# Capped attention and two MLPs on one core: first pair reordered on ScalarE, one tiny load moved to another queue, two pairs' sums moved behind accumulating transfers

## The chip, the cores and the metric

The kernel runs on one core of a Trainium2 chip. The metric is the device time of one execution in microseconds (us). Three runs of the kernel before took 581.67, 581.72 and 582.16 us, median 581.72. TensorE (PE in the profile), VectorE (DVE), ScalarE (ACT), GpSimd (POOL) and SyncE (SP) each run their own instruction stream in order; SP, ACT and POOL issue DMAs, each on its own queue.

## The reference

```
scores = cap * tanh((q @ k.T / sqrt(64)) / cap)          # 2 batches x 12 heads, 448 tokens
attn   = exp(scores - max); attn = attn / sum(attn)       # per row
x  = (attn @ v) as 896 x 768
h  = x @ w_in;  x = (h * sigmoid(1.702 h)) @ w_out        # 768 -> 2048 -> 768
xn = x / rms(x) * rms_g
y  = (silu(xn @ w_gate) * (xn @ w_val)) @ w_out2          # 768 -> 1536 -> 768
```

All inputs are float32. cap is one number that is loaded at run time.

## The kernel before

The attention works on 12 pairs of heads, `p` = 0 to 11; pairs 0 to 5 are the first batch, 6 to 11 the second. A pair's 448 keys are cut into three chunks of 128 and a rest of 64 ("the shared chunk", in which the two heads share the partitions). For each chunk TensorE makes scores (`scores`, `first_scores`, `scores_last`), ScalarE takes tanh (`tanh`, scale `tsc`, which VectorE makes from the loaded `cap` in `scale_by_cap`) and then exp in place (`exp`, scale `capt`). Chunks 0 and 1 stand in a tile `pa`, chunk 2 and the shared chunk in a tile `pb`. `outputs` multiplies with v into one PSUM tile, `copy_out` copies that to `z`.

Row sums: VectorE adds chunks 0 and 1 into `ts` (`add_two`); for pairs 1 to 9 GpSimd issues two accumulating DMAs (`add_third`, L340) that add the shared chunk into `ts`. `sums` (L349 to L368) lets TensorE multiply `ts` and then chunk 2 of `pb` with ones, 4 products for each stream (pairs without the DMAs have a third stream with `blk`), and VectorE transposes, takes reciprocals (`few`) and transposes back (`rs`). `spread` (L370) copies `rs` by four DMAs into a tile `r` with a row for each output row; SP issues all four, for pair 11 two of them go by ACT's queue. `norm` is three instructions on VectorE: `z` times `r` (L378), the rounded high half of the MLP's input `x` (L383), and the low half (L390). For pairs 10 and 11 ScalarE makes the high half (L385).

What sets the order is the program text: one loop over `p` (L435 to L504) in which each engine's instructions are written out, with tables `plan`, `RAW` and `NORMS` for the decoding and loading of weights and for the norms. Sums of a pair run two loops later (`done_`, L483), the last ones behind the loop's end. Buffers come from rotating pools: 3 `ts`, 4 `pb`, 2 `rs`, 5 `r`, 3 score tiles in PSUM, 1 output tile.

Behind it the MLP runs as one stream of TensorE products, three for each block (L568 high x high, L569 high x low, L570 low x high weights). Its first two columns use tokens 0 to 383 (pairs 0 to 5), the next two tokens 384 to 895, so pairs 6 to 11. Weights are loaded in units; each is decoded on ScalarE and VectorE into a `ring` tile, high half by L155 on ScalarE, low half by L160 on VectorE. Units 0 and 1 are ready early; unit 2's rest and unit 3 are decoded right behind the last norm. Four steps of the last norm and of unit 2 are handed to the MLP (`norm_last`) so that they stand in this order: `norm_mul(11)`, `norm_hi(11)`, L143 of unit 2, `norm_lo(11)`.

Of the kernel before, what the change touches and what calls it, by code (L numbers as in the profile page):

```python
# [12 lines left out]
ALU = mybir.AluOpType  # L13
# [4 lines left out]
def attn_moe_kernel(  # L18
# [14 lines left out]
    nc = tc.nc  # L33
# [9 lines left out]
    NC = 3  # L43
    NPR = B * NP
# [8 lines left out]
    capt = keep.tile([128, 1], F32, name="capt")  # L53
# [120 lines left out]
    def attention():  # L174
        with ExitStack() as actx:
# [15 lines left out]
            xs, raws, vs, pa, pb, zt, nr, ts_ = {}, {}, {}, {}, {}, {}, {}, {}  # L191
# [15 lines left out]
            cuts = [slice(0, S), slice(64, 192), slice(192, XW - S), slice(0, 64)]  # L207
# [86 lines left out]
            def exp(t):  # L294
                nc.scalar.activation(out=t, in_=t, func=AF.Exp, scale=capt)  # L295
# [31 lines left out]
                    nc.vector.tensor_copy(z, ps)  # L327

            LAST = range(1, NPR - 2)

            def add_two(p):
                ts_[p] = ap_.tile([128, 2, S], F32, tag="ts", name="ts", bufs=3)
# [2 lines left out]
            def add_third(p):  # L335
                if p == NPR - 1:
                    nc.vector.tensor_tensor(out=ts_[p], in0=ts_[p], in1=pb[p][:, 0:2], op=ALU.add)  # L337
                elif p in LAST:
                    for j in range(2):
                        nc.gpsimd.dma_start(  # L340
                            out=ts_[p][half[j], :, j * SH:(j + 1) * SH],
                            in_=pb[p][half[j], 2].rearrange("p (e s) -> p e s", e=2), accum_op=ALU.add,
                        )

            def sums(p):
                ps = ps_s.tile([128, 2, 512], F32, tag="s", name="s")[:, 0]
                streams = [ts_[p], *([] if p == NPR - 1 else [pb[p][:, 0:2]]), *([] if p in LAST else [None])]
                for n, some in enumerate(streams):
                    for e in range(2):  # L349
                        for j in range(2):  # L350
                            if some is None:
                                w, t = blk[:, 64 * j:64 * j + 32], pb[p][:, 2, e * SH:(e + 1) * SH]
                            else:
                                w, t = f(ones)[:, 0:32], some[:, e, j * SH:(j + 1) * SH]
                            r0 = 64 * j + 32 * e
                            nc.tensor.matmul(  # L356
                                out=ps[r0:r0 + 32, 0:SH], lhsT=w, rhs=t,
                                start=(n == 0), stop=(n == len(streams) - 1), skip_group_check=True,
                            )
                by_token = zrp.tile([128, SH // 32, 32], F32, tag="bt", name="bt", bufs=2)  # L360
                nc.vector.transpose(out=by_token.rearrange("p b t -> p (b t)"), in_=ps[:, 0:SH])
                few = zrp.tile([128, SH // 32], F32, tag="few", name="few", bufs=2)
                nc.vector.reciprocal(out=few, in_=by_token[:, :, 0])
                nr[p] = zrp.tile([128, SH], F32, tag="rs", name="rs", bufs=2)
                nc.vector.transpose(
                    out=nr[p], in_=few.rearrange("p (b o) -> p b o", o=1).to_broadcast([128, SH // 32, 32]),
                )
# [30 lines left out]
            nc.vector.memset(f(xA[0][:, 0, 0:S]), 1.0)  # L398
            ts = first_kq()
            nc.scalar.dma_start(out=ts[0], in_=q[0])  # L400
            nc.scalar.dma_start(out=capt, in_=cap.rearrange("(o n) -> o n", o=1).to_broadcast([128, 1]))
            nc.scalar.activation(out=tiny, in_=f(ones)[:, 0:1], func=AF.Tanh)
            nc.sync.dma_start(out=ts[1], in_=k[0, :, cuts[1]])
            nc.sync.dma_start(out=ts[2], in_=k[0, :, cuts[2]])
            nc.sync.dma_start(out=ts[3], in_=k[0, :, cuts[3]])
            constants()
            load_kq(1)
# [27 lines left out]
            for p in range(NPR + 1):  # L435
                load_kq(p + 3 if p < 2 else p + 4)
                load_v(p + 2)
                if p == 1:
                    load_kq(5)
                if p in RAW:  # L440
                    load_to(RAW[p])
                if p == 0:
                    for c in range(NC):
                        if c:
                            scores(0, c)
                            tanh(0, c)
                        else:
                            first_scores()
                        if c < 2:
                            exp(pa[0][:, c])  # L450
                    scores_last(0)
                    tanh(0, NC)
                    exp(pb[0])
                    outputs(0, (0,))
                    split_kq(1)
                    scores(1, 0)
                    outputs(0, (1,))
                elif p < NPR:
                    for c in range(NC):
                        if c and p == 1:  # L460
                            scores(p, c)
                        tanh(p, c)
                subtract = cast_kq(p + 2) if p + 2 < NPR else None
                for n in NORMS.get(p, (p - 6,) if p >= 6 else ()):
                    norm(n)
                decode(p, "b")
                if subtract:
                    subtract()
                decode(p, "c")
                if p >= 1:  # L470
                    if p == NPR:
                        sums(p - 2)
                        spread(p - 2)
                        add_third(p - 1)
                    if p < NPR:
                        outputs(p - 1, (NC,))
                        scores_last(p)
                        outputs(p - 1, range(NC) if p > 1 else (2,))
                    else:
                        outputs(p - 1)  # L480
                    if p < NPR:
                        copy_out(p - 1, "D")
                    done_ = p - 1 if p == 1 or p == NPR else p - 2  # L483
                    if done_ not in nr:
                        if p == NPR:
                            norm(8)
                        sums(done_)
                        if p == NPR:
                            copy_out(p - 1, "A")
                        spread(done_)  # L490
                        if p == NPR:
                            norm(9)
                if 1 <= p < NPR:
                    tanh(p, NC)
                    exp(pa[p])
                    exp(pb[p])
                if p < NPR:
                    add_two(p)
                    decode(p, "d")
                    if p < NPR - 1:  # L500
                        add_third(p)
                if p >= 1:
                    for c in range(NC):
                        scores(p + 1, c)  # L504
# [377 lines left out]
```

## Time and profile before

| what | value |
|---|---|
| median of three runs | 581.72 us |
| the profiled execution's own time | 581.83 us |
| its span in the profile | 580.0 us |
| granted TensorE clock | 1.00 |
| PE busy | 572.7 us, 99% |
| DVE busy | 411.9 us, 71% |
| ACT busy | 274.1 us, 47% |
| POOL busy | 59.1 us, 10% |
| chain that ended last, by engine | PE 94%, ACT 3%, DVE 1%, DMA 1% |

The share of busy time is a mean over stages with different limits. In the first 80 us, the attention, ACT has no idle time; from 84.6 us on only the MLP's products run on PE. A matmul's end in the trace is modelled, so starts are the better reading. PEld is the load of weights into PE.

### The profile page before, as it was taken

How to read it: one execution, taken by the hardware profiler on the slowest of the kernel's cores; microseconds unless marked ns; L12 is line 12 of the kernel's file. 1: busy time of each engine (PE TensorE's matmuls, PEld its weight loads, DVE VectorE, ACT ScalarE, POOL GpSimd, SP SyncE). 2: the span in 40 equal slices, each digit the busy share in tenths (PEclk: the TensorE clock that was granted, in tenths of full speed). 3: DMA queues.
4: the chain of work that ended last, by engine and by line, in shares of the span. 5: the costliest groups of instructions: out<-in, count | busy, mean ns of one | idle time of the engine just before them, and what ended most of it. 6: DMA issues, size and time to landing. Idle time of an engine off the chain costs nothing.

```text
span 580.0 us, 9373 instructions
## 1 busy us (share of the span) xinstructions
PE 572.7 (99%) x3842; PEld 493.2 (85%) x3842; DVE 411.9 (71%) x568; ACT 274.1 (47%) x369; POOL 59.1 (10%) x54
## 2 busy tenths in 40 slices
PE   8899999999999999999999999999999999999997
PEld 4566668989999998999998989889898998989887
DVE  4889997956653355656787999873687894778732
ACT  7999965755241355553444543442233431334300
POOL 0222300000000000000222013000222000222000
PEclk9999999999999999999999999999999999999999
DMA  8888643642624123233142414351132361222022
GB/s 300 245 218 198 123 113 90 201 135 94 206 62 157 56 71 127 98 124 120 61 148 70 164 59 160 110 164 54 55 114 104 111 217 56 61 108 105 1 92 99
DMA packets 60363, 70.31 MB, mean 121 GB/s; under 512 B 4128, under 2 KB 56480, under 8 KB 60320
## 3 DMA queue, kind: packets, MB, share of 16 engines
q1 hardware_dynamic: 57136, 67.04, 35.4%
q0 software_dynamic: 2592, 2.07, 3.0%
q10 hardware_dynamic: 592, 0.61, 0.4%
q8 instruction: 30, 0.49, 0.3%
q14 instruction: 13, 0.11, 0.1%
HBM read 62.13 MB, written 2.75 MB: 112 GB/s over the span
## 4 chain that ended last, share of the span: by engine, by line
PE 94%; ACT 3%; DVE 1%; DMA 1%; issue 0%; ACTq 0%
PE b L570 28%; PE b L569 28%; PE b L568 28%; PE v L314 4%; PE s L246 3%; PE s L356 1%; ACT pa L292 1%; PE s L273 1%; ACT pb L292 1%; ACT pb L295 1%; DMA capt<-in_cap 1%; ACT pa L295 1%; DVE ts L333 0%; DVE ts L337 0%; PE b L707 0%
## 5 line engine op out<-in xcount | busy, mean ns | idle before, releaser
L570 PE MATMUL b<-x,ring 128*128 128x384 f32 (+1 forms) x480 | 173.9, 362 | 0.0
L569 PE MATMUL b<-x,ring 128*128 128x384 f32 (+1 forms) x480 | 173.8, 362 | 0.0
L568 PE MATMUL b<-x,ring 128*128 128x384 f32 (+1 forms) x480 | 173.7, 362 | 0.0
L568 PEld LDWEIGHTS b<-x,ring 128*128 128x128 f32 x480 | 90.1, 188 | 9.9 <-issue 0.4
L569 PEld LDWEIGHTS b<-x,ring 128*128 128x128 f32 x480 | 90.1, 188 | 9.6
L570 PEld LDWEIGHTS b<-x,ring 128*128 128x128 f32 x480 | 90.1, 188 | 9.4
L160 DVE TENSOR_TENSOR ring<-dec,ring 128x768 fp32r<-128x768 f32 x68 | 77.1, 1136 | 28.1 <-ACT ring L155 28.1
L570 PE MATMUL b<-g,ring 128*128 128x512 f32 (+1 forms) x192 | 69.7, 363 | 0.0
L569 PE MATMUL b<-g,ring 128*128 128x512 f32 (+1 forms) x192 | 69.6, 363 | 0.0
L568 PE MATMUL b<-g,ring 128*128 128x512 f32 (+1 forms) x192 | 69.5, 362 | 0.0
L155 ACT ACTIVATE ring<-dec 128x768 fp32r<-128x768 f32 x66 | 55.2, 837 | 30.0 <-DVE dec L143 24.5
L143 DVE SCALAR_TENSOR_TENSOR dec<-raw,dec 128x768 uint32<-128x768 uint32 x68 | 66.8, 983 | 1.2
L137 DVE SCALAR_TENSOR_TENSOR dec<-raw,dec 128x768 uint32<-128x768 uint32 x68 | 64.7, 952 | 1.0
L129 ACT ACTIVATE dec<-raw 128x768 f32<-128x768 f32 x66 | 59.6, 904 | 5.0 <-issue 2.5
L570 PE MATMUL b<-uA,ring 128*128 128x512 f32 (+1 forms) x144 | 52.1, 362 | 0.0
L569 PE MATMUL b<-uA,ring 128*128 128x512 f32 (+1 forms) x144 | 52.1, 362 | 0.0
L568 PE MATMUL b<-uA,ring 128*128 128x512 f32 (+1 forms) x144 | 52.1, 362 | 0.0
L600 DVE TENSOR_TENSOR g<-gg,g 128x384 fp32r<-128x384 f32 (+1 forms) x32 | 20.0, 624 | 39.9 <-ACT g L597 39.8
L739 POOL TENSOR_TENSOR a<-a,gg 128x512 f32<-128x512 f32 (+1 forms) x18 | 29.2, 1621 | 187.1 <-DVE gg L732 160.0
L742 ACT ACTIVATE uA<-a 128x512 fp32r<-128x512 f32 (+1 forms) x24 | 13.9, 580 | 70.4 <-POOL a L739 52.1
L133 DVE TENSOR_SCALAR dec<-dec 128x768 uint32<-128x768 uint32 x68 | 39.4, 580 | 0.0
L569 PEld LDWEIGHTS b<-g,ring 128*128 128x128 f32 x192 | 36.0, 188 | 3.9
(89 smaller groups left out, 664.4 us busy)
## 6 DMA issues: line engine op xcount, KB each, us to landing
raw<-in_moe_w_out SPq DMA_DIRECT2D x20, 768.0 KB, 4.2
raw<-in_moe_w_in SPq DMA_DIRECT2D x16, 768.0 KB, 4.5
raw<-in_moe_w_gate SPq DMA_DIRECT2D x12, 768.0 KB, 4.2
raw<-in_moe_w_val SPq DMA_DIRECT2D x12, 768.0 KB, 4.2
raw<-in_moe_w_out SPq DMA_DIRECT2D x8, 512.0 KB, 3.6
v<-in_v SPq DMA_DIRECT2D x11, 256.0 KB, 5.2
r<-rs SPq DMA_DIRECT2D x46, 56.0 KB, 2.6
kq<-in_k SPq DMA_DIRECT2D x11, 224.0 KB, 4.6
```

Source lines behind the costliest of these rows:

```text
L129: nc.scalar.activation(out=f(d), in_=f(hi), func=AF.Copy, scale=2.0 ** -112)
L133: nc.vector.tensor_scalar(out=d, in0=d, scalar1=3, scalar2=None, op0=ALU.logical_shift_left)
L137: nc.vector.scalar_tensor_tensor(out=d, in0=hi, scalar=0x80000000, in1=d, op0=ALU.bitwise_and, op1=ALU.bitwise_or)
L143: nc.vector.scalar_tensor_tensor(out=d, in0=lo, scalar=29, in1=d, op0=ALU.logical_shift_right, op1=ALU.bitwise_or)
L155: nc.scalar.activation(out=t[:, 0], in_=f(dec_t[w][0]), func=AF.Copy)
L160: nc.vector.tensor_tensor(out=t[:, 1], in0=f(d), in1=f(t[:, 0]), op=ALU.subtract)
L314: nc.tensor.matmul(out=ps[32 * n:32 * n + 32, j, 0:SH], lhsT=w[:, d0:d0 + 32], rhs=t, start=not before, stop=len(before) == NC, skip_group ...
L568: nc.tensor.matmul(out=wide(o, b), lhsT=w0, rhs=x0, start=first, stop=False)
L569: nc.tensor.matmul(out=wide(o, b), lhsT=w0, rhs=x1, start=False, stop=False)
L570: nc.tensor.matmul(out=wide(o, b), lhsT=w1, rhs=x0, start=False, stop=last)
L600: nc.vector.tensor_tensor(out=gA[1].at(i, hb), in0=gg[0], in1=f(gA[0].at(i, hb)), op=ALU.subtract)
L739: eng.tensor_tensor(out=t[0], in0=t[0], in1=t[1], op=ALU.mult)
```

## The change

1. The first pair on ScalarE: tanh of chunk 1 now stands ahead of exp of chunk 0, and exp of chunk 1 behind tanh of chunk 2 and of the shared chunk. TensorE makes all three score chunks of pair 1 ahead of `outputs(0, (1,))`.
2. The load of `cap` moves from ACT's queue to SP's, second there, and the third piece of the first k (`ts[2]`, 128 KB) from SP's to ACT's, second there.
3. For pairs 8 and 9 GpSimd issues a third accumulating DMA, which adds chunk 2 (128 x 896 numbers) to `ts`; it names the same bytes as the two ahead of it and is issued once they have landed. `sums` of these pairs then has one stream of 4 products instead of two.
4. The sums of pair 8 move from loop 10 to loop 11, those of pair 9 from loop 11 behind those of pair 10 in loop 12. In loop 12 VectorE's `add_third(11)` and TensorE's `outputs(11, (0, 1))` come first. In loop 10 the condition on `done_` now gives 0, which is no longer in `nr`, so `sums(0)` and `spread(0)` run a second time there; nothing reads their result.

```diff
+            BOTH = (8, 9)
...
                             in_=pb[p][half[j], 2].rearrange("p (e s) -> p e s", e=2), accum_op=ALU.add,
                         )
+                    if p in BOTH:
+                        nc.gpsimd.dma_start(out=ts_[p], in_=pb[p][:, 0:2], accum_op=ALU.add)
...
-                streams = [ts_[p], *([] if p == NPR - 1 else [pb[p][:, 0:2]]), *([] if p in LAST else [None])]
+                streams = [ts_[p], *([] if p == NPR - 1 or p in BOTH else [pb[p][:, 0:2]]), *([] if p in LAST else [None])]
...
-            nc.scalar.dma_start(out=capt, in_=cap.rearrange("(o n) -> o n", o=1).to_broadcast([128, 1]))
+            nc.scalar.dma_start(out=ts[2], in_=k[0, :, cuts[2]])
...
-            nc.sync.dma_start(out=ts[2], in_=k[0, :, cuts[2]])
+            nc.sync.dma_start(out=capt, in_=cap.rearrange("(o n) -> o n", o=1).to_broadcast([128, 1]))
...
-                    for c in range(NC):
-                        if c:
-                            scores(0, c)
-                            tanh(0, c)
-                        else:
-                            first_scores()
-                        if c < 2:
-                            exp(pa[0][:, c])
+                    first_scores()
+                    scores(0, 1)
+                    tanh(0, 1)
+                    exp(pa[0][:, 0])
+                    scores(0, 2)
+                    tanh(0, 2)
                     scores_last(0)
                     tanh(0, NC)
+                    exp(pa[0][:, 1])
                     exp(pb[0])
                     outputs(0, (0,))
                     split_kq(1)
-                    scores(1, 0)
+                    for c in range(NC):
+                        scores(1, c)
                     outputs(0, (1,))
...
                     if p == NPR:
-                        sums(p - 2)
-                        spread(p - 2)
                         add_third(p - 1)
+                        outputs(p - 1, (0, 1))
+                        for n in (p - 2, p - 3):
+                            sums(n)
+                            spread(n)
...
-                        outputs(p - 1)
+                        outputs(p - 1, (2, NC))
...
-                    done_ = p - 1 if p == 1 or p == NPR else p - 2
+                    done_ = p - 1 if p in (1, NPR) else p - 3 if p == NPR - 1 else p - 2 if p < NPR - 2 else 0
```

In the program after the change the lines behind the edits stand 3 lower (L356 is L359, L378 is L381).

ScalarE at the start of the kernel, pair 0, before (`first` are the pieces of q and k, L262 the tanh of chunk 0 in two halves, L295 exp):

```order
L400 DMA first_93<-in_q 128x448
L401 DMA capt<-in_cap 128x1
L402 ACT_TABLE_LOAD
L402 ACTIVATE tiny<-ones 128x1
L205 DMA v<-in_v 128x512
L262 ACTIVATE pa<-s,tsc 128x2x224 x2
L295 ACTIVATE pa<-pa,capt 128x896
L292 ACTIVATE pa<-s,tsc 128x896
L295 ACTIVATE pa<-pa,capt 128x896
L292 ACTIVATE pb<-s,tsc 128x896
L292 ACTIVATE pb<-s,tsc 128x448
L295 ACTIVATE pb<-pb,capt 128x1344
```

The same place now:

```order
L403 DMA first_93<-in_q 128x448
L404 DMA first_95<-in_k 128x256
L405 ACT_TABLE_LOAD
L405 ACTIVATE tiny<-ones 128x1
L205 DMA v<-in_v 128x512
L262 ACTIVATE pa<-s,tsc 128x2x224 x2
L292 ACTIVATE pa<-s,tsc 128x896
L295 ACTIVATE pa<-pa,capt 128x896
L292 ACTIVATE pb<-s,tsc 128x896
L292 ACTIVATE pb<-s,tsc 128x448
L295 ACTIVATE pa<-pa,capt 128x896
L295 ACTIVATE pb<-pb,capt 128x1344
```

No exp follows directly on the tanh that it reads; the load of `cap` left this queue and a piece of k came.

TensorE at the attention's end, from the products of pair 10 with v on, before (`ts_1130` is pair 9, `ts_1235` pair 10, `ts_1336` pair 11):

```order
L314 MATMUL v_1269<-pb_1160,v_942 32x224 x8
L356 MATMUL s_1313<-ts_1130,ones_62 32x224 x4
L356 MATMUL s_1313<-pb_1054,ones_62 32x224 x4
L356 MATMUL s_1340<-ts_1235,ones_62 32x224 x4
L356 MATMUL s_1340<-pb_1160,ones_62 32x224 x4
L356 MATMUL s_1340<-pb_1160,blk_61 32x224 x4
L314 MATMUL v_1365<-pa_1258,v_1049 32x224 x16
L314 MATMUL v_1365<-pb_1261,v_1049 32x224 x16
L356 MATMUL s_1401<-ts_1336,ones_62 32x224 x4
L356 MATMUL s_1401<-pb_1261,blk_61 32x224 x4
```

The same place now (`ts_1024` is pair 8, `ts_1241` pair 10, `ts_1131` pair 9, `ts_1338` pair 11):

```order
L314 MATMUL v_1275<-pb_1162,v_942 32x224 x8
L359 MATMUL s_1319<-ts_1024,ones_62 32x224 x4
L314 MATMUL v_1343<-pa_1264,v_1050 32x224 x16
L359 MATMUL s_1360<-ts_1241,ones_62 32x224 x4
L359 MATMUL s_1360<-pb_1162,ones_62 32x224 x4
L359 MATMUL s_1360<-pb_1162,blk_61 32x224 x4
L359 MATMUL s_1384<-ts_1131,ones_62 32x224 x4
L314 MATMUL v_1343<-pb_1267,v_1050 32x224 x16
L359 MATMUL s_1419<-ts_1338,ones_62 32x224 x4
L359 MATMUL s_1419<-pb_1267,blk_61 32x224 x4
```

Sums of pair 8 stand where those of pair 9 stood, and those of pair 9 come behind those of pair 10 and half of pair 11's output.

VectorE at the same end, before, from the sums of pair 9 on (`rs_1328` is pair 9, `rs_1357` pair 10, `rs_1414` pair 11; `z_1105` pair 8):

```order
L365 STREAM_TRANSPOSE rs_1328<-few_1326 128x224
L333 TENSOR_TENSOR ts_1336<-pa_1258 128x896
L361 STREAM_TRANSPOSE bt_1353<-s_1340 128x224
L363 RECIPROCAL few_1355<-bt_1353 128x7
L365 STREAM_TRANSPOSE rs_1357<-few_1355 128x224
L337 TENSOR_TENSOR ts_1336<-ts_1336,pb_1261 128x896
L378 TENSOR_TENSOR z_1105<-z_1105,r_1227 128x448
L383 CAST x0_64<-z_1105 128x448
L390 TENSOR_TENSOR x1_65<-z_1105,x0_64 128x448
L361 STREAM_TRANSPOSE bt_1410<-s_1401 128x224
L363 RECIPROCAL few_1412<-bt_1410 128x7
L365 STREAM_TRANSPOSE rs_1414<-few_1412 128x224
```

The same place now, from the sums of pair 8 on (`rs_1328` is pair 8, `rs_1377` pair 10, `rs_1393` pair 9; `z_1106` pair 8; the transpose for pair 11 follows):

```order
L368 STREAM_TRANSPOSE rs_1328<-few_1326 128x224
L334 TENSOR_TENSOR ts_1338<-pa_1264 128x896
L338 TENSOR_TENSOR ts_1338<-ts_1338,pb_1267 128x896
L364 STREAM_TRANSPOSE bt_1373<-s_1360 128x224
L366 RECIPROCAL few_1375<-bt_1373 128x7
L368 STREAM_TRANSPOSE rs_1377<-few_1375 128x224
L364 STREAM_TRANSPOSE bt_1389<-s_1384 128x224
L366 RECIPROCAL few_1391<-bt_1389 128x7
L368 STREAM_TRANSPOSE rs_1393<-few_1391 128x224
L381 TENSOR_TENSOR z_1106<-z_1106,r_1330 128x448
L386 CAST x0_64<-z_1106 128x448
L393 TENSOR_TENSOR x1_65<-z_1106,x0_64 128x448
```

In both, the product of pair 9 comes next after the transpose for pair 11. Each `rs` is followed on SP's queue by its four spreading DMAs, in this order: pairs 9, 10, 11 before, pairs 8, 10, 9, 11 now. The product of pair 9 reads the tile that its spread fills.

## Rows read from the trace of the kernel before

**Rows 1.** Chain of waits, start of the kernel: start us, length us, what

```profile
1.20 3.98 DMA capt<-in_cap
```

**Rows 2.** Waits of PE from 74 us to the end: us in total, times, longest

```profile
PE s L356 <- DVE ts L337: 0.2, 1, 0.2
```

**Rows 3.** Timeline of ACT, 5 to 13 us: start, length, instruction, idle before it

```profile
5.66 1.16 ACT L262 ACTIVATE pa<-s,tsc 128x448 f32<-128x448 f32 x2 [2.48 <-DVE tsc L217]
...
7.80 0.99 ACT L292 ACTIVATE pa<-s,tsc 128x896 f32<-128x896 f32 x1
8.82 1.04 ACT L295 ACTIVATE pa<-pa,capt 128x896 f32<-128x896 f32 x1
9.77 1.52 ACT L292 ACTIVATE pb<-s,tsc 128x896 f32<-128x896 f32 x2
```

**Rows 4.** Timeline of SP, 0 to 2 us

```profile
0.75 0.39 SPq L403 DMA_DIRECT2D first<-in_k  x1
```

**Rows 5.** DMA issues, 0 to 2 us: count, KB, us from issue to landing

```profile
first<-in_k SPq DMA_DIRECT2D x1, 128.0 KB, 3.6
first<-in_k SPq DMA_DIRECT2D x1, 64.0 KB, 2.7
```

**Rows 6.** Waits of all engines, 60 to 84 us

```profile
PEld s L273 <- ACT pa L292: 0.8, 3, 0.3
```

**Rows 7.** Timeline of PE, 72 to 85 us (a product is two records)

```profile
78.55 0.56 PE L356 MATMUL s<-ts,ones 128*32 128x224 f32 x8
...
79.31 0.56 PE L356 MATMUL s<-ts,ones 128*32 128x224 f32 x8
...
80.44 1.70 PE L314 MATMUL v<-pa,v 128*32 128x224 f32 x32
81.96 1.48 PE L314 MATMUL v<-pb,v 128*32 128x224 f32 x32
83.67 0.59 PE L356 MATMUL s<-ts,ones 128*32 128x224 f32 x8 [0.23 <-DVE ts L337]
...
84.56 0.45 PE L568 MATMUL b<-x,ring 128*128 128x384 f32 x1
```

**Rows 8.** Timeline of ACT, 70 to 100 us

```profile
77.59 2.07 ACT L295 ACTIVATE pa<-pa,capt 128x1792 f32<-128x1792 f32 x1
...
91.14 0.58 ACT L385 ACTIVATE x<-z 128x448 fp32r<-128x448 f32 x1 [2.16 <-DVE z L378]
```

**Rows 9.** Timeline of DVE, 76 to 97 us

```profile
80.25 0.41 DVE L365 STREAM_TRANSPOSE rs<-few 128x224 f32<-128x224 f32 x1
...
82.56 1.05 DVE L337 TENSOR_TENSOR ts<-ts,pb 128x896 f32<-128x896 f32 x1
...
86.17 0.58 DVE L378 TENSOR_TENSOR z<-z,r 128x448 f32<-128x448 f32 x1
```

**Rows 10.** Timeline of SP, 80 to 90 us: the spreading DMAs

```profile
80.69 6.71 SPq L375 DMA_DIRECT2D r<-rs  x10
```

**Rows 11.** DMA issues, 85.5 to 86 us: one spreading DMA

```profile
r<-rs SPq DMA_DIRECT2D x1, 56.0 KB, 2.0
```

**Rows 12.** Timeline of POOL, 62 to 75 us: shared chunks of pairs 8 and 9

```profile
63.65 1.94 POOL L340 DMA_DIRECT2D ts<-pb  x2 [4.18 <-ACT pa L292]
70.12 2.05 POOL L340 DMA_DIRECT2D ts<-pb  x2 [4.53 <-ACT pa L292]
```

**Rows 13.** DMA issues, 62 to 66 us: the shared chunk of pair 8

```profile
ts<-pb POOLq DMA_DIRECT2D x2, 112.0 KB, 3.9
```

**Rows 14.** DMA queues over the whole span: packets, MB, share of 16 engines

```profile
q0 software_dynamic: 2592, 2.07, 3.0%
```

**Rows 15.** Waits of all engines, 90 to 103.3 us

```profile
ACT ring L155 <- DVE dec L143: 2.7, 1, 2.7
```

**Rows 16.** Timeline of DVE, 101.6 to 103.2 us: low half of unit 3

```profile
102.19 0.95 DVE L160 TENSOR_TENSOR ring<-dec,ring 128x768 fp32r<-128x768 f32 x1
```

**Rows 17.** Timeline of PE, 103.3 to 103.8 us: first use of that half

```profile
103.67 0.39 PE L570 MATMUL b<-x,ring 128*128 128x512 f32 x1
```

More of the change, by code (lines that the diff above doesn't have):

```diff
@@ L459, in attention @@
                     for c in range(NC):
-                        if c and p == 1:
-                            scores(p, c)
                         tanh(p, c)
```

## The prediction

> **What bounds the kernel now.** The page gives PE 99% busy, so I first asked where PE waits at all. The waits of PE from 74 us to the end hold one line, 0.2 us [rows 2]: from the first MLP product at 84.56 us [rows 7] the stream runs unbroken to the end. The time is therefore the start of that stream plus a fixed length, plus any wait that the change puts into it. I call times on this trace "the old clock".
>
> Then the chain of waits at the start: the load of `cap` takes 3.98 us from issue to landing [rows 1], and ScalarE's first tanh sits 2.48 us idle until VectorE has made `tsc` of it, starting at 5.66 us [rows 3]. From there ScalarE has no idle time up to pair 11's exp. In each loop PE's weight load for the last scores waits for ScalarE's tanh, three times in the last 24 us for 0.8 us together, up to 0.3 us each [rows 6]. So ScalarE paces the attention, and what is won at its start arrives at its end.
>
> Last, what stands behind the attention's end. Pair 9's norm product starts at 86.17 us [rows 9], pair 11's high half at 91.14 us [rows 8], and from there ScalarE and VectorE work without a wait for PE (none in the waits from 90 to 103.3 us; the longest is ScalarE for VectorE [rows 15]) until the low half of weight unit 3 is done at 102.19 + 0.95 = 103.14 us [rows 16]. PE first needs it at 103.67 us [rows 17]. That is 0.53 us of slack: whatever makes this chain later than PE's stream by more becomes a wait in the stream.
>
> **The start, ScalarE's order.** Exp directly behind its tanh starts after the tanh has ended: 7.80 + 0.99 = 8.79, exp at 8.82. Other neighbours overlap: 8.82 + 1.04 = 9.86, the next tanh at 9.77 [rows 3]. A dependent neighbour thus costs 0.03 + 0.09 = 0.12 us; there are three (behind chunk 0, chunk 1, `pb`), and the new order has none. Gain 0.36 us, if the scores are there.
>
> **The start, the load of `cap`.** On ACT's queue `cap` stood second, behind 224 KB of q, and landed at 1.20 + 3.98 = 5.18 [rows 1]. On SP's it stands second behind 64 KB, issued at 0.75 [rows 4], that take 2.7 us, so 3.45. The transfer now second there, 128 KB, takes 3.6 us from about 1.2 [rows 5], so 4.8 us. Bounds: 4.3 (half-way between 3.45 and 5.18) and 5.18 (no change). I take the nearest row, 4.8, a little earlier for the smaller load: gain 0.45 us, bounds 0 and 0.9. The 128 KB piece now waits behind q; if it lands after 5.3 us, the tanh that moved forward idles, which is why I don't take more. Start together: 0.8 us, bounds 0.3 and 1.3.
>
> A rule of the Trainium skill speaks against this term: "DMA: Bandwidth & Descriptors", section "Issuing engines are not separate DMA queues", says that DMAs of all engines run on the same 16 DMA engines and that spreading them over issuers saves only sequencer time. By it the move of `cap` is worth nothing and the sum is 584.9 us. The two second places above differ by 0.4 us in landing, which bears on it without deciding it, since the loads differ in size.
>
> **Loops 1 to 11.** The second `sums(0)` in loop 10 has 12 products where pair 8 had 8. Eight records, 4 products, take 0.38 us (78.55 and 79.31 are two such groups of 8 apart) [rows 7]. PE's wait of 0.27 us per loop covers most of it, about 0.1 us is left.
>
> The third transfer moves 448 KB. Bounds: a shared one of 112 KB lands 3.9 us after its issue [rows 13], so hardly under 4; the accumulating queue moved 2.07 MB in 3.0% of 16 engines' 580 us, 278 engine-us [rows 14], so 7.4 KB per engine-us, 3.9 us for 0.46 MB, on top of about 2.9 us that a shared one takes beside its data, so 6.8. I take 6.5, near the row of the same kind. Pair 8: shared ones issued at 63.65 [rows 12], landed by 68.8; third issued 69.4, landed about 76. Pair 9's follow on GpSimd at about 70.3 instead of 70.12 [rows 12], queue behind the third of pair 8 and land about 77; their own third goes out at 77.5 and lands at 84 (81.5 to 86).
>
> **The attention's end on PE.** Pair 10's output ends at 78.55 + 0.1. Sums of pair 8: 0.38, to 79.04. Then half of pair 11's output has to wait for its exp, 77.59 + 2.07 = 79.66 [rows 8], start 79.71; it takes 1.52 (80.44 to 81.96), pair 10's sums 1.13 (79.31 to 80.44), pair 9's 0.38, the other half 1.45 (81.96 to 83.67 without the wait), pair 11's sums 0.89 (83.67 to 84.56) [rows 7]. VectorE's added sum now ends near 82.7 instead of 82.56 + 1.05 = 83.61 [rows 9], so no wait there. Sum: 85.08, 0.5 us later than 84.56. If pair 9's third transfer lands at 84, PE stands 1.6 us in front of pair 9's sums, and the stream starts near 86.7; the next part hides that.
>
> **The norms.** This is the term that decides. Before, SP issued ten spreading DMAs at the end, 6.71 us, 0.67 each, the first at 80.69 [rows 10] right behind pair 9's `rs` (80.25 + 0.41) [rows 9]. The norm of pair 9 was served by the first four. Now pair 8's four stand first, from about 80.8 (its `rs` takes the same place), then pair 10's, and pair 9's are the ninth to twelfth. The twelfth goes out at 80.8 + 11 x 0.67 = 88.1 and lands 2.0 us later [rows 11], 90.1 us. VectorE can't take pair 9's product before; behind it on VectorE, in order, stand the norms of pairs 10 and 11 and the decoding of units 2 and 3. So the product starts at 90.2 instead of 86.17, 4.03 us later, and with it the low half of unit 3. Less the slack of 0.53, PE's stream loses 3.5 us; the 0.5 or 2.1 us of the later start are inside of this, not on top, since they move PE's need as well. Bounds: with issue and landing a tenth shorter (0.6 and 1.8) 2.6; with pair 9's transfer landing at 86 (deadline for pair 9's `rs` to reach SP in time: about 84.3) 5.2.
>
> **Sum.** 581.83 (the profiled execution's own time) - 0.8 + 3.5 = 584.5; it lies 0.1 above the median, so 584.4 us.
>
> **Rivals.** (a) Not slower: pair 9's spread isn't what the stream waits for. It needs pair 9's product by about 87.2 on the old clock (86.17, the slack and the later start of 0.5). Then 0.5 - 0.8 stays: 581.4 us. For it: the slack sits in one unit of weights, and SP may issue faster than ten rows of before show. Against: eight transfers stand ahead in one queue, and the twelfth would have to be out by 85.1. Chance 0.17; a gain over 0.2% (1.2 us, about what a measurement can tell from no change) needs the upper bound of the start as well, 0.05 of these.
>
> (b) Pair 9's third transfer lands late, at 86 or after, because its queue is shared with pair 8's and the engines with the spreading DMAs. Then pair 9's `rs` leads, each us behind 84.3 counts fully: 586.1 us at 86. For it: two waits for landings in a row that the kernel before didn't have. Chance 0.2.
>
> (c) The skill's rule on queues holds and `cap` lands no earlier: 584.9 us. Chance 0.13.
>
> (d) The load of `cap` gains its bound of 0.9 us and the norms their lower one: 581.7 - 1.3 + 2.6 = 583.0. It is the forecast's lower edge, not a case of its own.
>
> **How the numbers follow.** The forecast 584.4 has 0.5, with (d) as its edge; its own range is 583.0 to 585.6. With (b) and (c) slower has 0.83; (a) gives same 0.12 and faster 0.05. The range leaves out (a) and the end of (b): 582.8 to 586.6.
>
> **What would show it.** Right: ScalarE's first tanh near 5.2 us, no gaps behind tanh; ScalarE's last exp 0.8 us earlier; PE idle ahead of half of pair 11's output and of pair 9's sums; VectorE idle for about 2 us in front of pair 9's product with a spreading DMA as what ended it; PE waiting for VectorE in the fourth MLP column (pair 11's low half) and at unit 3. Wrong: no PE wait behind the first MLP product; pair 9's spread landed by 87; or a start that gains over 1.5 us.

## The result and the profile after

The changed kernel takes 586.49 us, median of four runs (585.49 to 586.89), against 581.76 us before (581.67 to 582.16): ratio 1.0076, 95% interval 1.0064 to 1.0089. It is slower by about 4.7 us. The prediction said 584.4 us, 582.8 to 586.6, slower: direction and mechanism hold, the size came out 2 us larger. The profiled execution took 586.89 us (span 585.1), the slowest of the four, so its trace shows about 0.4 us more than the median.

The chain of waits of the changed kernel from 81 us on (start us, length us, what):

```profile
81.44 1.09 DVE ts L338
...
83.13 0.41 DVE rs L368
...
84.07 1.56 SPq L378
...
88.23 0.59 SPq L378
...
88.87 2.31 DMA r<-rs
...
91.31 0.64 DVE z L381
...
107.43 0.88 DVE ring L160
108.36 0.50 PE b L573
```

VectorE makes pair 10's `rs`, SP issues the spreads of pairs 10 and 9 one after the other, the last of them lands at 91.18, and only then VectorE's product of pair 9 starts. From it the chain runs through the norms and the decoding to the low half of unit 3, for which TensorE waits at 108.36. In [rows 17] that product stands at 103.67: the stream is 4.69 us later there.

VectorE's timeline at the same place (start, length, instruction, idle before it and what ended it), which answers to [rows 9]:

```profile
79.95 0.41 DVE L368 STREAM_TRANSPOSE rs<-few 128x224 f32<-128x224 f32 x1
...
88.42 0.41 DVE L368 STREAM_TRANSPOSE rs<-few 128x224 f32<-128x224 f32 x1 [1.56 <-DMA r<-rs]
91.31 0.62 DVE L381 TENSOR_TENSOR z<-z,r 128x448 f32<-128x448 f32 x1 [2.48 <-DMA r<-rs]
```

These are `rs` of pairs 8 and 11 and the product of pair 9, now 91.31 instead of 86.17 (+5.14). `rs` of pair 11 waits too: it needs one of two buffers, which pair 10's spread was still reading.

TensorE at the attention's end, answering to [rows 7]:

```profile
78.48 0.56 PE L359 MATMUL s<-ts,ones 128*32 128x224 f32 x8
79.45 1.72 PE L314 MATMUL v<-pa,v 128*32 128x224 f32 x32 [0.42 <-ACT pa L295]
...
82.91 0.58 PE L359 MATMUL s<-ts,ones 128*32 128x224 f32 x8 [0.60 <-DMA ts<-pb]
...
85.61 0.44 PE L571 MATMUL b<-x,ring 128*128 128x384 f32 x1
```

It idles in front of half of pair 11's output and of pair 9's sums; the first MLP product starts 1.05 us later than 84.56. Behind it stand the waits of TensorE from 84.5 to 118.4 us (total, times, longest), where [rows 2] had none:

```profile
PE b L571 <- ACT x L388: 1.3, 1, 1.3
PE b L573 <- DVE ring L160: 1.3, 1, 1.3
PE b L572 <- DVE x L393: 0.2, 1, 0.2
```

They make 2.8 us. With the 1.05 us of the later start and some 0.9 us that the products lose around the waits they account, but for 0.1 us, for the 4.83 us by which the last MLP product ends later than before (581.54 instead of 576.71).

The start, ScalarE's timeline, answering to [rows 3] and [rows 8]:

```profile
5.55 1.16 ACT L262 ACTIVATE pa<-s,tsc 128x448 f32<-128x448 f32 x2 [2.38 <-DVE tsc L217]
6.75 1.01 ACT L292 ACTIVATE pa<-s,tsc 128x896 f32<-128x896 f32 x1
7.66 1.03 ACT L295 ACTIVATE pa<-pa,capt 128x896 f32<-128x896 f32 x1
...
12.24 1.01 ACT L292 ACTIVATE pa<-s,tsc 128x896 f32<-128x896 f32 x1
...
77.34 1.94 ACT L295 ACTIVATE pa<-pa,capt 128x1792 f32<-128x1792 f32 x1
```

No exp starts behind the end of the tanh that it reads, as forecast. But the first tanh starts only 0.11 us earlier (5.66 before), and pair 11's exp only 0.25 us earlier (77.59). The DMA issues of 1.0 to 1.5 us (KB, us to landing) say why, beside [rows 1] and [rows 5]:

```profile
first<-in_k ACTq DMA_DIRECT2D x1, 128.0 KB, 4.4
first<-in_k SPq DMA_DIRECT2D x1, 64.0 KB, 2.5
capt<-in_cap SPq DMA_DIRECT2D x1, 0.5 KB, 3.9
```

The load of `cap` still takes 3.9 us on the other queue. The piece of k that went behind q lands at about 5.6 us (1.20 + 4.4), against 4.8 before; TensorE's scores of chunk 1 start at 5.69 instead of 5.11, and in the chain of waits the tanh at 6.75 follows on them.

These 0.11 us are one pair of traces. Over all traces with the old place of the load (six) `cap` landed 3.4 to 4.0 us after its issue and the first tanh started at 5.25 to 5.66 us, over all with the new one (seven) 3.3 to 4.0 us and 5.11 to 5.64 us: the two overlap, and a gain of some tenths is neither shown nor excluded.

### The profile page after: what moved, and what is told of

Same layout as the page of the kernel before. It is cut to its first block, busy times and chain, and to the rows that moved or that the text cites. A ratio compares the mean times of both kernels' runs of the same rounds, so it can differ in the third digit from the quotient of the medians.

```text
span 585.1 us, 9407 instructions
## 1 busy us (share of the span) xinstructions
PE 574.5 (98%) x3850; PEld 493.8 (84%) x3850; DVE 413.0 (71%) x571; ACT 273.8 (47%) x369; POOL 61.1 (10%) x56
## 4 chain that ended last, share of the span: by engine, by line
PE 87%; ACT 5%; DMA 3%; DVE 2%; SPq 1%; issue 1%; DVEq 0%; ACTq 0%
PE b L573 27%; PE b L572 27%; PE b L571 27%; PE v L314 2%; DMA r<-rs 2%; PE s L246 2%; SPq L378 1%; DMA ts<-pb 1%; ACT pb L292 1%; ACT pb L295 1%; ACT pa L292 1%; PE s L359 1%; ACT pa L295 1%; PE s L273 0%; ACT dec L129 0%
## 5 line engine op out<-in xcount | busy, mean ns | idle before, releaser
L571 PEld LDWEIGHTS b<-x,ring 128*128 128x128 f32 x480 | 90.1, 188 | 11.6 <-ACT x L388 1.8
L573 PEld LDWEIGHTS b<-x,ring 128*128 128x128 f32 x480 | 90.1, 188 | 11.0 <-DVE ring L160 1.7
L572 PEld LDWEIGHTS b<-x,ring 128*128 128x128 f32 x480 | 90.1, 188 | 10.3 <-DVE x L393 0.7
```

Of the source, the lines that this page charges most:

```text
L571: nc.tensor.matmul(out=wide(o, b), lhsT=w0, rhs=x0, start=first, stop=False)
L572: nc.tensor.matmul(out=wide(o, b), lhsT=w0, rhs=x1, start=False, stop=False)
L573: nc.tensor.matmul(out=wide(o, b), lhsT=w1, rhs=x0, start=False, stop=last)
```

## The experiments

The theory: SP's queue and the place of pair 9's spread in it set pair 9's product, and what that product loses TensorE's stream loses. The rivals: TensorE's new order and the third transfers cost the time; a spread that comes late is late wherever it is issued. Ratios are to the kernel before, run on the same chip. The table has, for each kernel in which pair 9's spread was at issue, the product of pair 9 and the span, from its profiled run, beside what its runs took.

| kernel | product of pair 9, us | span, us | median of runs (range), us |
|---|---|---|---|
| before | 86.17 | 580.0 | 581.76 (581.67 to 582.16) |
| e11_swap_act | 85.85 | 579.7 | 581.62 (581.50 to 581.87) |
| e6_spread10_act | 88.30 | 582.1 | 584.88 (583.93 to 586.69) |
| e3_nine_first | 88.58 | 583.3 | 585.24 (584.98 to 585.91) |
| e10_swap_only | 89.12 | 583.0 | 584.65 (584.64 to 584.83) |
| e4_no_third9 | 89.57 | 583.4 | 585.70 (585.20 to 586.55) |
| e5_pair8_old | 89.62 | 583.2 | 585.31 (585.00 to 586.31) |
| e7_no_filler | 90.48 | 584.0 | 586.24 (584.95 to 587.15) |
| after | 91.31 | 585.1 | 586.49 (585.49 to 586.89) |
| e2_tail | 91.39 | 585.3 | 586.96 (586.75 to 587.10) |

But for one row the span follows the product: 580.0 + (product - 86.17) comes within about 0.3 us of it. The exception, e3, is explained below. The match is looser than it looks: TensorE's stream loses a little less than the product, and between the end of the last MLP product and the span's end the traces differ by 0.3 us (3.3 to 3.6).

The 95% intervals of the changed kernel and of each of its variants (e2 to e7) overlap, so their medians alone decide nothing between them; what these show is read from the traces. In the table only the kernel before, e11 and, just, e10 stand apart from it.

**e10_swap_only**: the order on SP alone, in the kernel before, with a third buffer for `rs` so that no transpose waits for one.

```diff
-                nr[p] = zrp.tile([128, SH], F32, tag="rs", name="rs", bufs=2)
+                nr[p] = zrp.tile([128, SH], F32, tag="rs", name="rs", bufs=3)
...
                         spread(p - 2)
+                        spread(p - 3)
...
-                        spread(done_)
+                        if p != NPR - 1:
+                            spread(done_)
```

> The kernel before with one thing moved: pair 9's four spreading DMAs are issued by SP behind pair 10's, in the last loop, and the tile rs has three buffers, so that none of the transposes waits for it. The start, the accumulating transfers, TensorE's order and the sums are those of before. Theory (SP's queue, 0.67 to 0.77 us for each issue, sets pair 9's norm product): SP starts with pair 10's spread at about 82.8, the eighth issue goes out at 87.5 to 88.2 and lands 2.0 to 2.3 us later, 89.5 to 90.5; pair 9's product starts there instead of 86.2 and unit 4's first use moves by 3.0 to 4.0 us: 584.8 to 585.8 us. Rival (the third transfers and TensorE's new order at the attention's end cost the time): no change, 581.8 us.

584.65 us, ratio 1.0050 [1.0037, 1.0063]. Its chain of waits:

```profile
82.60 0.46 SPq L375
...
86.30 0.60 SPq L375
...
86.94 2.15 DMA r<-rs
...
89.12 0.64 DVE z L378
```

Eight issues, 0.62 us apart, then a landing of 2.15 us: the product is 2.95 us later, the time 2.9 us longer. Two things add up here: SP starts at 82.60, when `rs` of pair 10 is there, instead of 80.69, and four more issues stand ahead. Of these 4.5 us some 1.2 are covered, since before the spread had landed by 85.0 and the product stood at 86.17 behind pair 11's transpose, and 0.35 come back by a shorter landing (2.15 instead of 2.5). Without a third transfer, without any new order on TensorE and with the old start, this one move gives more than half of the change's loss. The rival (581.8) falls.

**e11_swap_act**: the same place in the program, but another queue (the other edits as in e10).

```diff
-            def spread(p):
+            def spread(p, own=None):
...
-                        eng = nc.scalar if j and p == NPR - 1 else nc.sync
+                        eng = own or (nc.scalar if j and p == NPR - 1 else nc.sync)
...
                         spread(p - 2)
+                        spread(p - 3, nc.scalar)
```

> The same move as in e10, but pair 9's four spreading DMAs are issued by ScalarE, in front of its last copy into z, so that they don't stand behind pair 10's on SP's queue. Theory (the place in SP's queue costs, not that the spread comes in a later loop): ScalarE issues them from about 81 to 84, the last lands by 86.3, pair 9's product starts at 86.2 to 86.5, no wait behind the first MLP product: 581.6 to 582.2 us. Rival (a spread in the last loop is late wherever it is issued, because its transfers share the DMA engines with those of pair 10): product at 88 or later, 583.5 us or more.

581.62 us, 0.9997 [0.9989, 1.0006]. The timelines of ScalarE, SP and VectorE:

```profile
80.38 3.38 ACTq L375 DMA_DIRECT2D r<-rs  x4
82.35 4.70 SPq L375 DMA_DIRECT2D r<-rs  x6
85.85 0.58 DVE L378 TENSOR_TENSOR z<-z,r 128x448 f32<-128x448 f32 x1
```

ScalarE's queue was free: it issues pair 9's spread from 80.38 on, as soon as `rs` is there, so that in time nothing is put off; SP's spread of pair 10 runs beside its end. The product starts right behind the transpose of pair 11, with no idle time, and the loss is gone. So what costs is standing in SP's queue behind a spread that has first to wait for its own `rs`. That the move in the program costs by itself, or that the two spreads hinder each other on the DMA engines, doesn't show here, though they overlap only in part. The same was not run in the changed kernel.

**e5_pair8_old**: pair 8 out of SP's queue.

```diff
-            BOTH = (8, 9)
+            BOTH = (9,)
...
-                    done_ = p - 1 if p in (1, NPR) else p - 3 if p == NPR - 1 else p - 2 if p < NPR - 2 else 0
-                    if done_ not in nr:
+                    done_ = p - 1 if p in (1, NPR) else p - 2 if p < NPR - 1 else 0
+                    if done_ not in nr and not p == NPR - 1:
```

> The changed kernel with pair 8 as before (no third transfer, sums in loop 10, spread there) and pair 9 put off as in the change; the second sums(0) and spread(0) are gone. Theory: SP has only pair 10's and pair 9's spreads ahead of pair 9's product, but it starts on them only when rs of pair 10 is there, at about 83; the eighth issue goes out near 88.4 and lands at 90.5, 0.7 us earlier than in the changed kernel: 585.5 to 586.1 us. Rival (the number of transfers that stand ahead in all counts, twelve or eight): 0.75 us for each of four, 3 us less, 583.5 us.

585.31 us, 1.0068 [1.0054, 1.0081]; the median is 0.2 below the theory's range, and the 583.5 of counting all transfers alike is far off.

```profile
83.00 6.47 SPq L378 DMA_DIRECT2D r<-rs  x10
...
89.62 0.63 DVE L381 TENSOR_TENSOR z<-z,r 128x448 f32<-128x448 f32 x1 [2.31 <-DMA r<-rs]
```

With pair 8's spread gone SP starts on pair 10's at 83.00 instead of 83.57. In the changed kernel pair 8's four issues were over at 82.8, before `rs` of pair 10 was there: they are off the chain. The rest of the 1.69 us between the two products is mostly one long issue of the changed kernel (1.56 us at 84.07), which e5 doesn't have.

**e3_nine_first**: sums and spread of pair 9 ahead of those of pair 10.

```diff
-                        for n in (p - 2, p - 3):
+                        for n in (p - 3, p - 2):
```

> The changed kernel with pair 9's sums and spread ahead of pair 10's in the last loop. Theory (spread queue): pair 9's norm product waits for its spread, which stands ninth to twelfth on SP's queue; now it stands fifth to eighth, so the product starts about 1.7 us earlier than the 91.31 us of the changed kernel, and the time falls by as much, to about 584.8 us, although PE now waits longer for pair 9's third transfer and starts the MLP about 1 us later (86.7 instead of 85.61). Rival (late transfer): the loss comes from PE's wait for the third transfer and the later start of the MLP; then the time rises by about 1 us, to 587.5.

585.24 us, 1.0063 [1.0048, 1.0078]. TensorE's and VectorE's timelines:

```profile
82.61 0.96 PE L359 MATMUL s<-ts,ones 128*32 128x224 f32 x16 [1.55 <-DMA ts<-pb]
88.58 0.58 DVE L381 TENSOR_TENSOR z<-z,r 128x448 f32<-128x448 f32 x1
91.08 0.63 DVE L381 TENSOR_TENSOR z<-z,r 128x448 f32<-128x448 f32 x1 [0.83 <-DMA r<-rs]
```

Pair 9's product waits for no spread of its own any more, but now TensorE stands in front of pair 9's sums until the third transfer has landed, and what follows on VectorE, the product of pair 10, waits for the spread that is last. With 0.83 added, 88.58 fits the span of 583.3. The wait moves from pair 9 to pair 10; about 1.2 us of the loss goes, by the medians.

**e6_spread10_act**: pair 10's spread on ScalarE's queue.

```diff
-                        eng = nc.scalar if j and p == NPR - 1 else nc.sync
+                        eng = nc.scalar if (j and p == NPR - 1) or p == NPR - 2 else nc.sync
```

> The changed kernel with pair 10's four spreading DMAs on ACT's queue instead of SP's. Theory (spread queue): pair 9's four go out as soon as its sums are inverted (about 84.7), land near 89.2 instead of 91.18, and pair 9's product starts 2 us earlier: time about 584.5. Rival (late transfer, or landing times set by the 16 shared DMA engines and not by the issuing queue): no change, 586.5, within 0.4.

584.88 us, 1.0058 [1.0040, 1.0077], with runs from 583.93 (the profiled one) to 586.69.

```profile
83.13 3.23 ACTq L378 DMA_DIRECT2D r<-rs  x4
...
87.90 0.41 DVE L368 STREAM_TRANSPOSE rs<-few 128x224 f32<-128x224 f32 x1 [1.49 <-DMA r<-rs]
88.30 0.63 DVE L381 TENSOR_TENSOR z<-z,r 128x448 f32<-128x448 f32 x1
```

The product is 3.0 us earlier than in the changed kernel and so is the span; the profiled run is the fastest of four, and the median falls by 1.6 us. What stands in front of it now is the transpose of pair 11, which waits for its buffer: the next limit, 2.1 us above the kernel before.

**e4_no_third9** and **e7_no_filler**: without pair 9's third transfer; without the second `sums(0)` and `spread(0)`.

```diff
-            BOTH = (8, 9)
+            BOTH = (8,)
```

```diff
-                    if done_ not in nr:
+                    if done_ not in nr and not p == NPR - 2:
```

> The changed kernel without the third accumulating transfer of pair 9 (its sums take two streams again), order unchanged. Theory (spread queue): the first MLP product starts 0.2 us earlier (0.6 of waiting less 0.4 of products), pair 9's spread keeps its place, and the time stays within 0.4 us of 586.5. Rival (late transfer): PE's wait and what the 448 KB take from the spreading DMAs cost 1 to 2 us, so the time falls to 584.5 to 585.5.

> The changed kernel without the second run of the sums and the spread of pair 0 in loop 10. Theory (spread queue): these stand before the end and cover nothing and block nothing there; 12 products fewer give PE 0.1 us at most behind its wait, the time stays within 0.3 us of 586.5. Rival (filler): the four extra spreading DMAs (landed at 80.2 to 80.8, beside a weight load) and the 12 products push the end: the time falls by 1 us or more, to 585.5 or less.

585.70 us, 1.0070 [1.0055, 1.0085], and 586.24 us, 1.0078 [1.0060, 1.0096]. VectorE in e4:

```profile
89.57 0.63 DVE L381 TENSOR_TENSOR z<-z,r 128x448 f32<-128x448 f32 x1 [1.95 <-DMA r<-rs]
```

With no transfer to wait for, the product still waits for the spread. The third transfer is not the main cause. The time is 0.8 us below that of the changed kernel, between the theory's range and the rival's and in neither, and within the two kernels' spread of runs: a part of that size isn't excluded. The filler costs nothing that the runs can tell from no change; in the traces the exps of pairs 10 and 11 stand 6.33 us apart with it (the changed kernel) and 6.18 without it (e7), as before (6.17).

**e2_tail**: the change with the start of before (both edits of the start taken out, and nothing else).

> The changed kernel with the start of the kernel before: both edits of the start are taken out, all the rest is as in the change. If the parts add up, the start is worth what it showed alone (0.4 us faster to 0.5 us slower) and the time is 586.2 to 587.0 us. Rival (the end sets the time whatever the start does, since the wait for the spreading DMAs swallows it): the same 586.5 us as the changed kernel, pair 9's product at the same 91.3 us.

586.96 us, 1.0089 [1.0075, 1.0102]; the intervals of this and the changed kernel overlap, so the two readings aren't told apart. Its profiled run shows something else, in TensorE's and VectorE's timelines and in a row of the windows (us, busy time of each engine, granted clock, DMA share, GB/s):

```profile
85.36 0.98 PE L359 MATMUL s<-ts,ones 128*32 128x224 f32 x8 [2.60 <-DMA ts<-pb]
86.08 2.68 PE L314 MATMUL v<-pb,v 128*32 128x224 f32 x32
...
87.08 0.41 DVE L368 STREAM_TRANSPOSE rs<-few 128x224 f32<-128x224 f32 x1
...
91.39 0.63 DVE L381 TENSOR_TENSOR z<-z,r 128x448 f32<-128x448 f32 x1 [0.55 <-DMA r<-rs]
```

```profile
85.30:88.70 3.40, 3.33 (x41) 1.37 (x42) 2.16 (x6) 0.00 (x0) 0.00 (x0) 0.51 0.32 71
```

Here pair 9's third transfer was issued at 80.38 and landed at 85.23, 2.5 us later than in the changed kernel: the way of rival (b) of the prediction, though 0.8 us short of its 86. Its `rs` comes at 87.08 and leads pair 9's spread, and the product is nearly where SP's queue had put it.

**e1_order**, **e1_head**, **e8_cap_first**: parts of the start in the kernel before: the interleave; the interleave with the move of `cap`; the interleave with `cap` first on SP's queue.

The first two are the two edits of the start as the change's diff shows them; e8 has, beside the interleave,

```diff
-            nc.scalar.dma_start(out=capt, in_=cap.rearrange("(o n) -> o n", o=1).to_broadcast([128, 1]))
             nc.scalar.activation(out=tiny, in_=f(ones)[:, 0:1], func=AF.Tanh)
+            nc.sync.dma_start(out=capt, in_=cap.rearrange("(o n) -> o n", o=1).to_broadcast([128, 1]))
             nc.sync.dma_start(out=ts[1], in_=k[0, :, cuts[1]])
```

> The kernel before with ScalarE's order of pair 0 alone, all loads as before. Theory (a dependent neighbour costs 0.12 us, three of them): 0.36 us less, 581.35 us; the first tanh stays at 5.66. Rival (the moved tanh of chunk 1 idles for its scores and gives the gain back): 581.7.

> The kernel before with the changed start alone (ScalarE's order in pair 0, cap on SP's queue, a piece of k on ACT's); everything from loop 1 on as before. Theory (the start arrives at the end, the loss is all in the spread order): in the changed kernel pair 1's first tanh started 0.40 us earlier (12.24 instead of 12.64), so about 581.35 us, 0.4 below the kernel before. Rival (the start costs something that shows only later, through the later landing of k, kq and v by 0.5 to 1.4 us): 581.7 or more.

> ScalarE's order of pair 0, and cap as the very first DMA on SP's queue, the pieces of k behind it as before. Theory (the load of cap takes its 3.9 us whatever stands ahead of it: 3.98 on ACT's queue behind 224 KB, 3.88 on SP's behind 64 KB): it lands near 4.65, the first tanh starts at about 5.1 to 5.2, 0.5 us earlier than 5.66, and the time is about 580.9. Rival (what stands ahead in the queue and the 16 shared engines set its landing): it lands at about 3.5 and the first scores become the limit, 580.6 or less; or the first k piece becomes late by as much, and nothing is gained over ScalarE's order alone (581.35).

e1_order 581.75 us, 0.9999 [0.9990, 1.0008]; e1_head 581.42 us, 0.9996 [0.9987, 1.0004]; e8 583.08 us, 1.0022 [1.0014, 1.0031]. ScalarE's first tanh of pair 1 in e1_order:

```profile
12.14 1.02 ACT L292 ACTIVATE pa<-s,tsc 128x896 f32<-128x896 f32 x1
```

The same in the kernel before:

```profile
12.64 0.99 ACT L292 ACTIVATE pa<-s,tsc 128x896 f32<-128x896 f32 x1
```

From 12.64 to 12.14 the interleave gives 0.50 us, 0.46 of it behind the first tanh, and with the move of `cap` beside it (e1_head) the same tanh starts at 12.22: the move adds nothing in this pair of traces. Either is too small to show over the runs, which spread by 1.1 to 1.3 us. In e8 the DMA issues, and TensorE's and ScalarE's timelines:

```profile
first<-in_q ACTq DMA_DIRECT2D x1, 224.0 KB, 3.9
...
first<-in_k SPq DMA_DIRECT2D x1, 64.0 KB, 3.7
capt<-in_cap SPq DMA_DIRECT2D x1, 0.5 KB, 3.4
```

```profile
4.99 1.86 PE L256 MATMUL s<-first,first 64*128 64x224 f32 x8 [0.84 <-DMA first<-in_k]
6.14 1.38 ACT L262 ACTIVATE pa<-s,tsc 128x448 f32<-128x448 f32 x2 [3.44 <-PE s L256]
```

`cap` lands at 4.15, 1.0 us earlier, but q and k then take about 1 us longer (3.0 and 2.5 in e1_order), TensorE waits for k and the first tanh for TensorE. ScalarE's load of v (256 KB) also went out earlier there, at 1.27 instead of 1.74, so that which of the two delays q and k isn't shown.

**e9_best**: an attempt at a kernel faster than before: the interleave, and `add_third(11)` ahead of the sums of pair 10, to take away TensorE's wait of [rows 2].

```diff
                     if p == NPR:
+                        add_third(p - 1)
                         sums(p - 2)
                         spread(p - 2)
-                        add_third(p - 1)
```

> The kernel before with ScalarE's order of pair 0 and, in the last loop, VectorE's added sum of pair 11 ahead of the sums of pair 10; no third transfers, pair 9's spread first as before. Theory: 0.36 us from the start, and PE's wait of 0.23 us ahead of pair 11's sums goes (the added sum ends near 82.3 instead of 83.61): 581.1 us. Rival (pair 9's norm product and what is behind it are the next limit at once, the slack there being 0.3 to 0.5 us): the second part gives nothing, 581.35.

581.50 us, 0.9994 [0.9985, 1.0003]: not to be told from before. In its profiled run (582.05, among the slower ones) the wait of [rows 2] is gone, but ScalarE waited for scores at the start:

```profile
7.49 1.01 ACT L292 ACTIVATE pa<-s,tsc 128x896 f32<-128x896 f32 x1 [0.75 <-PE s L246]
```

The first products of chunk 1's scores stand 0.75 us apart there, up to 7.23 us, where in the kernel before the same two stand 0.37 apart.

So no kernel tried here is shown to beat the one before.

## Why the prediction was right, and where its sizes were off

**The range.** 586.49 lies 0.1 us inside 582.8 to 586.6 and outside 583.0 to 585.6, the forecast's own range (for whose upper end no sum is given). The part in which it lies was added for rival (b), whose late transfer the changed kernel's trace doesn't show. So the direction and the mechanism were worked out; that the range holds is luck.

**The mechanism.** Right. Pair 9's product waits for the twelfth spreading DMA at the end, behind it the norms and the decoding of unit 3 are late, and TensorE waits at two places. The rows that were named came: VectorE idle about 2 us in front of that product with a spreading DMA as releaser (2.48), TensorE's wait in the fourth column (1.3 for pair 11's high half, where its low half was named, 0.2) and at unit 3 (1.3).

**The start, forecast 0.8.** Mis-sized: in the profiled run the first tanh gained 0.11, not 0.45, by `cap`; the interleave gave about its 0.36 (0.46 in e1_order; in the changed kernel 12.64 - 12.24 less 0.11 = 0.29, since TensorE's scores came later there; the piece of k landed at about 5.6, behind the 5.3 from which the prediction saw a risk). At pair 11's exp 0.25 us were left, since the filler took 0.15 of them. `cap` was sized by a 128 KB piece that stood second, but a load of 0.5 KB isn't faster there: 3.9 us in the changed kernel, and 3.3 to 4.0 over the traces, as much as second on ScalarE's queue. That is the result that rival (c) had, by the page of the Trainium skill ("DMA: Bandwidth & Descriptors", section "Issuing engines are not separate DMA queues"): by it the queue brings the landing no gain, and these traces show none beyond their spread. The same passage of the page leaves the time on the sequencer as what a second issuer saves, and calls it usually small: between e10 and e11 it makes 3 us here, since on SP the spread stands behind another one's wait for its `rs` and its four issues.

**Twelve issues from 80.8 us, landed at 90.1.** Right in kind, too short, and put together wrongly. On the new start's clock the forecast was 89.4 for the product; it came at 91.31, 1.9 us later: 0.55 because the start gave 0.25 and not 0.8, and some 1.4 because of this term. Pair 8's four issues, from 80.39 to 82.8, are not on the chain: SP then idles until `rs` of pair 10 is there at 83.5. The true sum is 83.57, the time from the first to the eighth issue, and the landing. Against e10, where the same eight issues start at 82.60: `rs` of pair 10 comes 0.97 later, since half of pair 11's output and `add_third(11)` now stand ahead of it; the eighth issue starts 5.30 instead of 4.34 us behind the first, because one, at 84.07, took 1.56; the landing takes 2.31 instead of 2.15. Together 2.09 of the 2.19 between the two products (91.31 and 89.12). The remaining 2.95 are what the order on SP costs in e10.

**The slack of 0.53.** Nearly right at its place (the product of [rows 17] moved 4.69 where VectorE moved 5.14), but behind it the last MLP product moved 0.14 more. Another 0.3 of the span's 5.1 stand behind that product, where nothing of the change is.

**The third transfers.** Landed at 75.1 and 82.8, forecast 76 and 84; TensorE's wait in front of pair 9's sums 0.60 instead of 1.6. Hidden, as said. Rival (b) didn't hold in the changed kernel's profile; e2's, with the transfer landed at 85.23, shows that its wait can lead.

**The buffer of `rs`.** Missed: two buffers, and pair 11's transpose had to wait 1.56 us for pair 10's spread. It cost nothing there, since pair 9's product was later still, and is the next limit in e6.

**Rival (a), not slower.** Its point was a product by about 87.2. SP issued some 0.62 us apart at best, so the eighth of the issues that start at 82.6 in e10 could not have landed by then; e11 meets it with a second queue and is not slower.

Open: the long issues. Among the spreading DMAs issued between 80 and 90 us nine of the fourteen traces have one of 1.0 to 1.6 us: 1.56 in the changed kernel, 1.08 in the kernel before, 1.44 in e1_order, 1.42 and 1.33 on ScalarE's queue in e11 and e6; e3, e4, e5, e9 and e10 have none there. Each of the nine landed late, 2.4 to 3.2 us after its issue where most take 2.0. So the 0.96 us that the long issue puts into the changed kernel's chain are not shown to belong to the change. The changed kernel and most of its variants spread by 0.9 to 2.8 us from run to run, e10 by 0.2 and e2 by 0.35; whether these issues are the reason wasn't settled.

## What to carry to other kernels

Here a spread of four small DMAs costs its queue 2.5 us and 2 us more to land. Where a late consumer reads it, ask when the spread ahead of it in that queue can start, count the issues from there, and look for another engine that is idle there, before its place is given to work that is needed later. A change that lets sums wait for a cheaper form saves nothing on an engine that then waits for something else, if what is put off feeds an in-order engine with the deadline behind it. A load's time second in a queue is read from a load of its own size, not from its neighbour's.

## What the runs showed of the hardware that was not expected

After TensorE had been idle for 2.60 us in e2 the granted clock of the next 3.4 us was 0.51, its lower level of 1.2 GHz, and half of pair 11's output took 2.68 us instead of 1.50; behind idle times of 0.60 (after) and 1.55 us (e3) it stayed at 1.00. With a load of 0.5 KB put first on SP's queue (e8), and one of 256 KB on ScalarE's issued 0.47 us earlier, two loads of 64 and 224 KB took about 1 us longer to land. A spreading DMA that ran beside the 448 KB transfer in e2 landed 4.3 us after its issue, but such late landings are not its mark: spreading DMAs issued between 80.7 and 82.5 us took 2.5 to 3.1 us in the kernel before and up to 3.7 in e9, without a third transfer, and most of those issued from 84 us on took 1.9 to 2.3.

At the start TensorE's score products run at half their later pace for a time that differs from trace to trace: in e9 products of 448 columns stand 0.75 us apart up to 7.23 us, in the kernel before 0.37 from 5.11 on, with the same loads in both. The windows of the profile give a granted clock of 1.00 there, so the reason isn't shown; but ScalarE's second tanh starts at 7.49 in e9 and at 6.67 in e1_order, which has the same order, and that is more than the interleave gives.
